# The order of additions and operand sums at the change of passes, and of the left-over rows' weights

## The chip, the cores and the metric

The kernel runs on one core of one Trainium2 chip. A core has five engines, each with its own instruction queue: TensorE (PE, matmuls; PEld is its weight load), VectorE (DVE), ScalarE (ACT), GpSimd (POOL) and SyncE (SP). The last two mostly issue DMAs here; ScalarE issues a few. The metric is the time of one execution on the device in microseconds (us). The profile comes from one such execution.

## The reference

The inputs are x (8 x 5696 x 128), h (5696 x 128) and four weights. First comes a long causal convolution along the sequence, written with FFTs, then a "wave" mixing over tokens and a channel product:

```
y  = irfft(rfft(x, 2S) * rfft(h, 2S))[:, :S]          # S = 5696
th = y @ w_theta
zr, zi = y * cos(th), y * sin(th)
u  = y + w_tok_r @ zr + w_tok_i @ zi                   # token products, S x S weights
out = u + relu(u @ w_ch)
```

Nearly three quarters of the time is the line with the two S x S products.

## The kernel before

**The stages.** The FFT convolution and the phases (theta, sine, cosine, products) take the first part of the span. From about 540 us on, the token mixing runs. The contraction over tokens, together with the real and imaginary part, is cut into two halves p = 0 and p = 1, called *passes* here. Within a pass, the 5696 = 2 x 2816 + 64 rows of the result are visited in 22 *visits* tt = 0 to 21; one visit makes the four 128-row by 512-column tiles of rows tt and 22 + tt, for both halves of the batch. One more visit, written tt = None, makes the last 64 rows: the *left-over* visit. Pass 0 goes 0 to 20, None, 21; pass 1 goes 0, None, 1 to 21 (`pairs`).

**A visit.** The contraction of one pass is 11 operand tiles j = 0 to 10 (`bts`). A visit runs through them in four *parts* (`stretches`) of j = 0 to 2, 3 to 5, 6 to 8 and 9 to 10. Ordinary visits use Strassen's seven products instead of eight: each has its own PSUM bank (tags m0 to m6, constants M2, M6, M7, M5, M1, M3, M4), and the seven are run in the order M3, M4, M5, M2, M1, M7, M6 (`ORDER`, L1290). After the last part, VectorE adds each bank with its sign to the result tiles c11, c12, c21, c22 (L1297), and c goes to a buffer in HBM (pass 0, `cp_hbm`) or to the output stage (pass 1).

**Operand sums.** Strassen's products need sums of the operand blocks b11, b12, b21, b22. For each j there are five, numbered k = 0 to 4 in `sum_ops` (L833 to 838; all show as L835): M3 = b12 - b22, M4 = b21 - b11, M1 = b11 + b22, and then b12 and b21 are overwritten by b11 + b12 and b21 + b22. The first visit of each pass (in pass 0 the second too) is *plain* (`plain`, branch `classic`): eight products with the raw blocks (L1210), so the sums can be made while it runs. The last two of a j must wait until the plain visit has read that j. The left-over visit needs only M3 and M4 of each j (L1178, with the raw b11 and b22); the visits after it need all five. In pass 1 the sums wait in a list `sums_1`, from which `late_sums(n)` issues the first n.

**Weights.** They come as f32 pairs through a ring of six slots, by POOL (L680, `load_w`, called from `pump`, which goes on when `prepare` marks a chunk as read). `prepare(i)` makes the weights of part i: block transposes on VectorE from the ring (`w_t`, L894), then Strassen's sums of weights (`w_sum`, L903). Usually part i + 1 is prepared as part i begins, and at the end of a visit interleaved with the final additions (`woven`), unless the left-over visit comes next. The transposed weights have five slots, the sums four.

**Output stage.** `u_stage` has two halves. `first`: ScalarE casts c to ub (L971), TensorE transposes it into utp (L974), ScalarE copies that to SBUF (L976). `second`: TensorE multiplies by w_ch into v (L981), VectorE makes c + relu(v) (L983), SP stores it. Both PSUM tiles use the bank "misc". The stages of finished tiles wait in `spread`; `aside(first_of, second_of)` issues one half each, once per part.

**Orders.** Tile, the layer below, plans each engine's order from the order of issue and its own cost model. In two stretches of the mixing the order of VectorE is kept as written (`manual_schedule`, `ordered`, L1117 to 1122): at the start of pass 0, and in pass 1 from the first plain part until visit 1 begins. The rest of the text calls these written-out orders. The other engines' orders are always planned.

**At the change of passes before.** In the last plain part of pass 1, six sums are issued ahead of the products (L1241), then the four result additions (L1253), then all sums left (L1269, six), then four more enter the list. In the left-over visit the stage's first half stands ahead of each part's matmuls, its second half behind them, and all remaining sums are issued behind the first part (L1183).

Of the kernel before, what the change touches and what calls it, by code (L numbers as in the profile page):

```python
# [22 lines left out]
def kernel(  # L23
# [624 lines left out]
    first_of = {}  # L648
# [83 lines left out]
    M2, M6, M7, M5, M1, M3, M4 = range(7)  # L732
# [100 lines left out]
    def sum_ops(bt):  # L833
        b11, b12, b21, b22 = (bt[q] for q in (M2, M6, M7, M5))
        return [lambda f=f, x=x: f(*x) for f, x in (  # L835
            (nc.vector.tensor_sub, (bt[M3], b12, b22)), (nc.vector.tensor_sub, (bt[M4], b21, b11)),
            (nc.vector.tensor_add, (bt[M1], b11, b22)), (nc.vector.tensor_add, (b12, b11, b12)),
            (nc.vector.tensor_add, (b21, b21, b22)))]
# [209 lines left out]
    def late_sums(n):  # L1048

        for _ in range(min(n, len(sums_1))):  # L1050
            sums_1.pop(0)()

    stretches = []
    for k, (p, tt, c) in enumerate(chunks):
# [58 lines left out]
            return a  # L1113
        return a, step

    nxt, second, st = None, None, {}
    ordered = ExitStack()  # L1117
    for i, (k, p, tt, j0, s0, nj) in enumerate(stretches):
        if (p, tt, j0 + s0) in ((0, 0, 0), (1, 0, 0)):
# [20 lines left out]
        if p and first_of_pair and tt == 1:  # L1140
            nc.vector.tensor_add(zl[2], zl[0], zl[1])
        if p and tt == 0:
            sums_1 += [op for j in range(nj) for op in sum_ops(bts[j0 + s0 + j])[:3]]
        held = a if i else None
        a, nxt = nxt, None if i == 1 else prepare(i + 1, not woven)
        if woven:
            nxt, step = nxt
        def aside(first_of, second_of):
            nonlocal second
            if first_of and spread and (p == 1 or (tt > 0 and not end_of_pair)):  # L1150
                where_bg["tags"] = ("c2", "c3") if j0 + s0 == TJ else ("red", "mag")
                _, first, second = spread.pop(0)
                with tc.issue_after(sides["late"].ins) if p == 0 and tt == 1 else ExitStack():
                    first()
                    if len(spread) > 1:
                        spread[1][0]()
            if second_of and second is not None:
                second()
                second = None

        if tt is None:
            if p:
                aside(True, False)
            if first_of_pair:
                q = M1 if p else M3
                ps = mps.tile([P, 512], F32, tag=f"m{q}", name=f"m{q}")
                c_last = addend_last(p)
            a1, a2, sa = a
            terms = ((sa, M2, a2, M4), (a1, M3, sa, M5))
            for j in range(nj):  # L1170
                jj = j0 + s0 + j
                for r in range(2):
                    b = [x[:, r, :] for x in bts[jj]]
                    st_ = jj == 0 and r == 0
                    sp_ = jj == NJ - 1 and r == 1 and zl is None
                    for k_ in range(2):
                        for h, t in enumerate(terms):
                            nc.tensor.matmul(ps[64 * h:64 * h + 64], t[2 * k_][:, j, :64, r], b[t[2 * k_ + 1]],  # L1178
                                             start=st_ and k_ == 0, stop=sp_ and k_ == 1)
            if p:  # L1180
                aside(False, True)
            if p == 1:
                late_sums(len(sums_1))  # L1183
            if end_of_pair:
                if zl is not None:
                    wl = wl_room()
                    nc.sync.dma_start(wl[:, :64], wl_hbm[:, NT - 1, :64])
                    for h in range(2):
                        nc.tensor.matmul(ps[64 * h:64 * h + 64], wl[:, :64], zl[h], start=False, stop=True)
                c, c0 = c_last  # L1190
                nc.vector.tensor_add(c, c0, ps)
                finish(p, NT - 1, 0, c)
            continue
# [43 lines left out]
                            sum_some(1)  # L1237
            continue
        if classic:
            if p and end_of_pair:  # L1240
                late_sums(6)  # L1241
            for n in range(4):
                for j in range(nj):
                    product(a, j0 + s0 + j, j, n, range(2))
                    if p == 0 and (n * nj + j) % 4 != 3:
                        sum_some(1)
                if end_of_pair and n % 2:
                    (c12, z12), (c21, z21), (c11, z11), (c22, z22) = cs
                    out_of = (((c11, z11, 0), (c12, z12, 1)), ((c21, z21, 2), (c22, z22, 3)))[n // 2]
                    for h, (c, z, m_) in enumerate(out_of):  # L1250
                        if p:
                            nc.tensor.matmul(ms[m_], wl[n // 2], zl[h], start=False, stop=True)
                            nc.vector.tensor_tensor(c, z, ms[m_], op=add)  # L1253
                            continue
                        if n == 1:
                            nc.tensor.matmul(ms[m_], ident_bf, z, start=False, stop=True)
                        else:
                            for b in range(4):
                                nc.tensor.matmul(ms[m_][:, b * D:(b + 1) * D], z[:, b, :], ident_bf,
                                                 start=False, stop=(b == 3))  # L1260
                        nc.scalar.activation(c, ms[m_], AF.Copy)
                aside(n == 0, n == 2)
            if end_of_pair and woven:
                for n_ in range(7):
                    step(n_)
            if p == 0:
                done["used"] = tt * (j0 + s0 + nj)
            else:
                late_sums(len(sums_1) if end_of_pair else 3)  # L1269
                sums_1 += [op for j in range(nj) for op in sum_ops(bts[j0 + s0 + j])[3:]]  # L1270
        else:
            left = {}
            if zl is not None and end_of_pair:
                left = {M5: (wl[0], zl[1]), M7: (wl[0], zl[2]),
                        M2: (wl[1], zl[0]), M6: (wl[1], zl[2])}
            if end_of_pair:
                (c12, z12), (c21, z21), (c11, z11), (c22, z22) = cs
                sums = {M3: ((c12, z12, add), (c22, z22, add)), M4: ((c11, z11, add), (c21, z21, add)),
                        M5: ((c11, c11, ALU.subtract), (c12, c12, add)),
                        M2: ((c21, c21, add), (c22, c22, ALU.subtract)),  # L1280
                        M1: ((c11, c11, add), (c22, c22, add)),
                        M7: ((c11, c11, add),), M6: ((c22, c22, add),)}
            while owed and owed[0][0] < j0 + s0 + nj:
                sum_some(1)
            for n, q in enumerate(ORDER):
                sum_some(1)
                for j in range(nj):
                    jj = j0 + s0 + j
                    for r in range(2):
                        nc.tensor.matmul(ms[q], a[q][:, j, :, r], bts[jj][q][:, r, :],  # L1290
                                         start=(jj == 0 and r == 0),
                                         stop=(jj == NJ - 1 and r == 1 and q not in left))
                if q in left:
                    nc.tensor.matmul(ms[q], left[q][0], left[q][1], start=False, stop=True)  # L1294
                if end_of_pair:
                    for c, z, op in (sums[q][::-1] if i + 1 == len(stretches) and q == M5 else sums[q]):
                        nc.vector.tensor_tensor(c, z, ms[q], op=op)  # L1297
                    if i + 1 == len(stretches):
                        if n == 4:
                            ends = [u_stage(t, h, c, P) for (t, h), (c, _) in zip(where, cs)]  # L1300
                            ends[0][1]((f"m{M3}", f"m{M5}", "yy0"))
                        elif n == 5:
                            ends[1][1]((f"m{M4}", f"m{M2}", "yy1"))
                        elif n == 6:
                            ends[0][2]()
                            ends[2][1]((f"m{M1}", f"m{M3}", "yy2"))
                            ends[1][2]()
                            ends[3][1]((f"m{M7}", f"m{M5}", "yy3"))
                            ends[2][2]()
                            ends[3][2]()  # L1310
                    if woven:
                        for n_ in {1: (0, 1), 2: (2,), 3: (3,), 4: (4,), 5: (5,), 6: (6,)}.get(n, ()):
                            step(n_)
                aside(n == 1, n == 4)
# [38 lines left out]
```

## Time and profile before

| what | value |
|---|---|
| median of 3 runs | 2037.92 us (2035.97 to 2045.31) |
| profiled execution | 2040.29 us, span 2038.5 us |
| TensorE busy | 1944.0 us, 95% |
| VectorE busy | 1539.8 us, 76% |
| GpSimd busy | 966.7 us, 47% |
| ScalarE busy | 638.9 us, 31% |

In rows of the timeline the first number is the start in us from the span's start, the second the length of the group, then the engine, line and operation, output <- input, the number of instructions and, in brackets, the idle time before the first and what ended it. Rows of waits give the waiting engine and what it waited for, the total in us, the number of times and the longest. The span is from the first to the last instruction; the execution's own time is a little longer.

The change of passes on TensorE lies at 1215 us (visit 21 of pass 0 ends, the plain visit of pass 1 begins), the left-over visits near 1171 and 1260 us.

### The profile page before, as it was taken

How to read it: one execution, taken by the hardware profiler on the slowest of the kernel's cores; microseconds unless marked ns; L12 is line 12 of the kernel's file. 1: busy time of each engine (PE TensorE's matmuls, PEld its weight loads, DVE VectorE, ACT ScalarE, POOL GpSimd, SP SyncE). 2: the span in 40 equal slices, each digit the busy share in tenths (PEclk: the TensorE clock that was granted, in tenths of full speed). 3: DMA queues.
4: the chain of work that ended last, by engine and by line, in shares of the span. 5: the costliest groups of instructions: out<-in, count | busy, mean ns of one | idle time of the engine just before them, and what ended most of it. 6: DMA issues, size and time to landing. Idle time of an engine off the chain costs nothing.

```text
span 2038.5 us, 42418 instructions
## 1 busy us (share of the span) xinstructions
PE 1944.0 (95%) x16121; PEld 1077.9 (53%) x16297; DVE 1539.8 (76%) x2817; ACT 638.9 (31%) x936; POOL 966.7 (47%) x1769
## 2 busy tenths in 40 slices
PE   7789898799999999999999998999999999999998
PEld 5688887654444444444444443444444444444444
DVE  8877877557778787887867668768677786777767
ACT  6788787762233323332300000111111111111111
POOL 8334213284353545454566454553545445354450
PEclk9999999899999999999999999999999999999999
DMA  9999988899798989999999798896978879788793
GB/s 155 163 173 145 161 164 231 244 261 178 157 180 173 174 173 162 181 173 181 165 173 152 122 247 206 137 154 126 153 136 141 151 126 155 130 151 142 134 157 84
DMA packets 510349, 334.77 MB, mean 164 GB/s; under 512 B 186631, under 2 KB 463111, under 8 KB 510055
## 3 DMA queue, kind: packets, MB, share of 16 engines
q0 software_dynamic: 322368, 157.47, 60.6%
q1 hardware_dynamic: 181792, 163.03, 27.3%
q10 hardware_dynamic: 5984, 11.54, 1.6%
q8 instruction: 128, 2.10, 0.4%
q14 instruction: 77, 0.63, 0.1%
HBM read 374.82 MB, written 95.24 MB: 231 GB/s over the span
## 4 chain that ended last, share of the span: by engine, by line
PE 66%; DMA 3%; DVE 3%; issue 1%; POOL 0%; ACT 0%; DVEq 0%
PE m L1290 61%; DMA ring<-in_moe_w_tok_i_dram 3%; DVE c L1297 1%; PE utp L974 1%; PE v L981 1%; PE m L1294 1%; DVE wt L894 1%; DMA ring<-in_moe_w_tok_r_dram 1%; PE theta_ps L564 0%; DVE b L835 0%; PE tpz L922 0%; PE m L1178 0%; POOL ring L680 0%; ACT ub L971 0%; DVE c L983 0%
## 5 line engine op out<-in xcount | busy, mean ns | idle before, releaser
L680 POOL DMA_DIRECT2D ring<-in_moe_w_tok_i_dram x720 | 388.6, 545 | 663.0 <-DVE wt L894 583.8
L680 POOL DMA_DIRECT2D ring<-in_moe_w_tok_r_dram x720 | 387.2, 546 | 130.2 <-DVE wt L894 70.9
L894 DVE STREAM_TRANSPOSE wt<-ring 128x384 f32<-128x384 f32 (+2 forms) x720 | 359.9, 525 | 115.6 <-PE m L1290 81.3
L1290 PE MATMUL m<-b,wt 128*128 128x512 bf16 x1604 | 384.8, 379 | 3.8 <-DVE wt L894 1.7
L1290 PEld LDWEIGHTS <-wt 128*128 128x128 bf16 x1804 | 176.0, 98 | 215.4 <-DVE wt L894 3.9
L1297 DVE TENSOR_TENSOR c<-c,m 128x512 f32<-128x512 f32 x412 | 265.9, 671 | 0.4 <-PE m L1290 0.4
L976 ACT ACTIVATE ring<-utp 128x512 bf16<-128x512 bf16 x85 | 50.7, 597 | 577.5 <-PE utp L974 577.5
L453 PE MATMUL ps<-r_u,uv_t 128*128 128x128 f16 x1024 | 117.3, 220 | 5.4 <-DVE g__1416 L460 2.0
L1210 PE MATMUL m<-b,wt 128*128 128x512 bf16 x471 | 113.0, 387 | 8.8 <-DMA b<-z_hbm 4.8
L971 ACT ACTIVATE ub<-c 128x512 bf16<-128x512 f32 x88 | 55.1, 628 | 201.0 <-DVE c L1253 118.6
L454 PE MATMUL ps<-r_v,uv_t 128*128 128x100 f16 x1024 | 115.3, 209 | 0.1
L153 POOL DMA_DIRECT2D x<-in_x_dram x128 | 99.5, 783 | 20.4 <-POOL x L151 14.9
L454 PEld LDWEIGHTS <-uv_t 128*128 128x128 f16 x1024 | 100.8, 99 | 5.9 <-issue 4.9
L433 DVE TENSOR_TENSOR uv_t<-xs,hs 128x2048 f16<-128x2048 f16 x77 | 91.5, 1223 | 16.3 <-DMA hs<-hf_hbm 9.2
L453 PEld LDWEIGHTS <-uv_t 128*128 128x128 f16 x1024 | 100.9, 98 | 2.3 <-DVE uv_t L438 2.1
L431 ACT ACTIVATE xs<-ps 128x1024 f16<-128x1024 f32 x96 | 90.8, 972 | 30.1 <-PE ps L270 14.3
L1210 PEld LDWEIGHTS <-wt 128*128 128x128 bf16 x528 | 51.5, 100 | 71.0 <-issue 12.6
L566 ACT ACTIVATE red<-theta_ps,magic 128x512 f32<-128x512 f32 (+1 forms) x46 | 31.6, 687 | 155.6 <-PE theta_ps L564 86.2
L270 PEld LDWEIGHTS <-w_t 64*128 64x128 f16 x3240 | 56.3, 98 | 31.0 <-issue 22.7
L924 ACT ACTIVATE ring<-tpz 128x512 bf16<-128x512 bf16 (+1 forms) x46 | 27.5, 597 | 134.0 <-PE tpz L922 120.2
L250 PE MATMUL ps<-f_t,x 89*128 89x180 f16 x512 | 62.0, 250 | 2.2 <-DVE a L257 1.8
L983 DVE SCALAR_TENSOR_TENSOR c<-v,c 128x512 f32<-128x512 f32 x88 | 60.1, 684 | 4.8 <-PE v L981 4.5
(2925 smaller groups left out, 3733.9 us busy)
## 6 DMA issues: line engine op xcount, KB each, us to landing
ring<-in_moe_w_tok_r_dram POOLq DMA_DIRECT2D x352, 96.0 KB, 4.4
ring<-in_moe_w_tok_i_dram POOLq DMA_DIRECT2D x352, 96.0 KB, 5.0
ring<-in_moe_w_tok_r_dram POOLq DMA_DIRECT2D x352, 80.0 KB, 4.6
ring<-in_moe_w_tok_i_dram POOLq DMA_DIRECT2D x352, 80.0 KB, 3.9
cp_hbm<-c SPq DMA_DIRECT2D x88, 256.0 KB, 2.5
c<-cp_hbm SPq DMA_DIRECT2D x88, 256.0 KB, 4.5
out_dram<-c SPq DMA_DIRECT2D x88, 256.0 KB, 4.7
hs<-hf_hbm SPq DMA_DIRECT2D x77, 256.0 KB, 3.5
```

The source lines that it names most:

```text
L153: nc.gpsimd.dma_start(x16[p0:p1, e, n0:n0 + 16, :HD], bass.AP(tensor=src.tensor, offset=src.offset + (p0 * N2 + n0) * D + dh * HD, ap=[[N2 ...
L250: nc.tensor.matmul(ps[:, i // 2, (i % 2) * 2 * K1:(i % 2 + 1) * 2 * K1], lhs(q + i), f1_t[:NB], start=True, stop=True)
L431: nc.scalar.activation(xs[:, :, :, :ck], ps, AF.Copy)
L433: nc.vector.tensor_tensor(uv[:, :, :, c0:c0 + ck], xs.rearrange("p e d k -> p e (d k)").unsqueeze(1).to_broadcast([P, 2, 2, HD * CK]), hv. ...
L453: nc.tensor.matmul(o, u_t[:, at:at + P], r_u, start=True, stop=False)
L454: nc.tensor.matmul(o[:, 2 * NP:], v_t[:, at:at + P], r_v, start=False, stop=True)
L680: nc.gpsimd.dma_start(wb[32 * i:32 * i + 32, :ng, :nj * 64], bass.AP(tensor=a.tensor, offset=a.offset + row0 * S + p * H + i * QR + j0 * 6 ...
L894: nc.vector.transpose(wt.rearrange("p j t r -> p (j t r)").bitcast(F32).rearrange("p (j g t) -> p g j t", j=TJ, g=4)[:, :ng, :nj], wb[:, : ...
L983: nc.vector.scalar_tensor_tensor(c[:m], v[:m], 0.0, c[:m], op0=ALU.max, op1=ALU.add)
L1210: nc.tensor.matmul(ms[n // 2 * 2 + h], a[n][:, j, :, r], bts_of[p][jj][n % 2 * 2 + h][:, r, :], start=(n % 2 == 0 and jj == 0 and r == 0), ...
L1290: nc.tensor.matmul(ms[q], a[q][:, j, :, r], bts[jj][q][:, r, :], start=(jj == 0 and r == 0), stop=(jj == NJ - 1 and r == 1 and q not in left))
L1297: nc.vector.tensor_tensor(c, z, ms[q], op=op)
```

## The change

It has three parts.

1. In the last plain part of pass 1 the six sums ahead of the products and the flush behind them are gone. Two sums are issued between the two pairs of result additions. In the left-over visit two are issued behind each part; ahead of a part, `needed` issues what that part must have (k < 2 there). Visit 1 issues two ahead of each part while any are left, and `needed` sees that all five are made up to that part's last j. With the sums as listed, that gives: two between the additions, two behind each of the left-over parts, three more ahead of the fourth, two ahead of visit 1's first part and the last ahead of its second.
2. In the left-over visit of pass 1 the output stage's first half moves behind the matmuls of the part's first j, and its v gets the bank of M7 instead of "misc".
3. In pass 0, in the last part of visit 20, part two of the left-over visit is prepared after the product M1 and its additions, ahead of M7 and M6, and kept in `ahead`; before, it was prepared when the left-over visit's first part began. Its ring loads are issued with it.

```
 def late_sums(n):
     for _ in range(min(n, len(sums_1))):
-        sums_1.pop(0)()
+        sums_1.pop(0)[2]()
+def needed(hi, k):
+    while any(o[0] < hi and o[1] < k for o in sums_1):
+        late_sums(1)
+def sums_of(j, lo, hi):
+    return [(j, k, f) for k, f in enumerate(sum_ops(bts_of[1][j]))][lo:hi]
...
     if p and tt == 0:
-        sums_1 += [op for j in range(nj) for op in sum_ops(bts[j0 + s0 + j])[:3]]
+        sums_1 += [op for j in range(nj) for op in sums_of(j0 + s0 + j, 0, 3)]
+    if p and tt is None:
+        needed(j0 + s0 + nj, 2)
+    elif p and tt:
+        late_sums(2)
+        needed(j0 + s0 + nj, 5)
-    a, nxt = nxt, None if i == 1 else prepare(i + 1, not woven)
+    a, nxt = nxt, None if i == 1 else ahead.pop(i + 1) if i + 1 in ahead else prepare(i + 1, not woven)
-    def aside(first_of, second_of):
+    def aside(first_of, second_of, *banks):
...
-                first()
+                first(*banks)
...
     if tt is None:
-        if p:
-            aside(True, False)
...
+            if p and j == 0:
+                aside(True, False, ("misc", f"m{M7}", None))
         if p:
             aside(False, True)
-        if p == 1:
-            late_sums(len(sums_1))
+            late_sums(2)
...
     if classic:
-        if p and end_of_pair:
-            late_sums(6)
...
                         nc.vector.tensor_tensor(c, z, ms[m_], op=add)
+                        late_sums(2 if n == 1 and h else 0)
...
-            late_sums(len(sums_1) if end_of_pair else 3)
-            sums_1 += [op for j in range(nj) for op in sum_ops(bts[j0 + s0 + j])[3:]]
+            late_sums(0 if end_of_pair else 3)
+            sums_1 += [op for j in range(nj) for op in sums_of(j0 + s0 + j, 3, 5)]
...
             if end_of_pair:
+                if n == 4 and p == 0 and not woven and i + 2 < len(stretches):
+                    ahead[i + 2] = prepare(i + 2)
```

More of the change, by code (lines that the diff above doesn't have):

```diff
@@ L1114, in prepare @@
         return a, step
-    nxt, second, st = None, None, {}
+    nxt, second, st, ahead = None, None, {}, {}
     ordered = ExitStack()
```

## The prediction

> **What bounds the kernel now.** I began with the page: span, busy shares and the chain that ended last.
>
> ```profile
> span 2038.5 us, 42418 instructions
> PE 1944.0 (95%) x16121; PEld 1077.9 (53%) x16297; DVE 1539.8 (76%) x2817; ACT 638.9 (31%) x936; POOL 966.7 (47%) x1769
> PE 66%; DMA 3%; DVE 3%; issue 1%; POOL 0%; ACT 0%; DVEq 0%
> ```
>
> TensorE is busy 95% of the span and carries 66% of the chain. So a microsecond is won only where TensorE itself stands still or runs slowly, and the next view is what TensorE waits for, once from 1160 to 1300 us (both edited places) and once from 1300 us to the end.
>
> ```profile
> PE utp L974 <- ACT ub L971: 3.4, 1, 3.4
> PE m L1210 <- DMA b<-z_hbm: 1.8, 2, 1.1
> PE m L1178 <- DVE out__18210 L903: 1.1, 1, 1.1
> ...
> PE utp L974 <- ACT ub L971: 0.9, 2, 0.7
> PE v L981 <- ACT uts L976: 0.2, 1, 0.2
> ```
>
> The first three rows are the early window, the last two all that it waits for after 1300 us: 1.1 us in 738. What is won at the change of passes is therefore kept to the end, as long as that order holds. The busy times by stretch (length; then PE, PEld, DVE, ACT, POOL; then the granted clock) show the place:
>
> ```profile
> 1247.00:1253.00 6.00, 4.20 (x20) 1.85 (x20) 6.00 (x12) 0.00 (x0) 3.71 (x8) 1.00 0.86 142
> 1253.00:1256.40 3.40, 3.37 (x16) 1.34 (x14) 3.40 (x9) 0.00 (x0) 1.30 (x3) 1.00 1.14 152
> 1256.40:1259.70 3.30, 0.00 (x0) 0.00 (x0) 3.30 (x7) 0.61 (x1) 0.00 (x0) 0.88 0.21 35
> 1259.70:1265.50 5.80, 5.73 (x28) 2.31 (x28) 5.07 (x10) 2.17 (x5) 1.06 (x2) 0.50 0.01 3
> ```
>
> VectorE is full while TensorE has nothing to do for 3.3 us, and then TensorE works 5.8 us at a granted clock of 0.50. The instructions of VectorE there, in order of time:
>
> ```profile
> 1253.90 0.34 DVE L903 TENSOR_TENSOR out__18917<-wt 128x384 bf16<-128x384 bf16 x1
> 1254.16 3.69 DVE L835 TENSOR_TENSOR b<-b 128x1024 bf16<-128x1024 bf16 x6
> 1257.78 2.47 DVE L1253 TENSOR_TENSOR c<-c,m 128x512 f32<-128x512 f32 x4
> 1260.17 3.69 DVE L835 TENSOR_TENSOR b<-b 128x1024 bf16<-128x1024 bf16 x6
> 1263.78 0.63 DVE L894 STREAM_TRANSPOSE wt<-ring 128x192 f32<-128x192 f32 x2
> 1264.44 0.36 DVE L903 TENSOR_TENSOR out__18991<-wt 128x384 bf16<-128x384 bf16 x1
> 1266.13 0.69 DVE L983 SCALAR_TENSOR_TENSOR c<-v,c 128x512 f32<-128x512 f32 x1 [1.33 <-PE v L981]
> ...
> 1274.10 0.69 DVE L983 SCALAR_TENSOR_TENSOR c<-v,c 128x512 f32<-128x512 f32 x1 [2.59 <-PE v L981]
> 1274.71 1.49 DVE L894 STREAM_TRANSPOSE wt<-ring 128x384 f32<-128x384 f32 x3
> ```
>
> and of TensorE, with two rows of ScalarE:
>
> ```profile
> 1255.77 0.59 PE L1252 MATMUL m<-zl,wl 128*128 128x512 bf16 x2
> 1259.77 0.61 PE L974 MATMUL utp<-ident_bf,ub 128*128 128x128 bf16 x4 [3.41 <-ACT ub L971]
> 1270.22 0.41 PE L1178 MATMUL m<-b,out__19043 128*64 128x512 bf16 x1 [0.35 <-DVE out__19043 L903]
> ...
> 1271.56 0.38 PE L1178 MATMUL m<-b,out__19043 128*64 128x512 bf16 x2
> 1271.78 0.38 PE L1178 MATMUL m<-b,wt 128*64 128x512 bf16 x2
> ...
> 1273.60 0.40 PE L981 MATMUL v<-w_ch_sb,ring 128*128 128x128 bf16 x4
> 1273.93 0.41 PE L1178 MATMUL m<-b,out__19096 128*64 128x512 bf16 x1
> ...
> 1277.34 0.38 PE L1290 MATMUL m<-ring,wt 128*128 128x512 bf16 x1 [0.16 <-DVE wt L894]
> ```
>
> ```profile
> 1259.09 0.63 ACT L971 ACTIVATE ub<-c 128x512 bf16<-128x512 f32 x1 [118.61 <-DVE c L1253]
> 1260.48 0.60 ACT L976 ACTIVATE ring<-utp 128x512 bf16<-128x512 bf16 x1 [0.76 <-PE utp L974]
> ```
>
> TensorE ends the plain visit at 1255.77 + 0.59 = 1256.36. Six operand sums (1254.16, 3.69 us) hold VectorE until the four additions start at 1257.78; the first output tile needs one, ScalarE's copy needs that, and the transposes on TensorE need the copy. The first part's matmuls, whose operand was ready at 1254.24, stand behind those transposes. The left-over rows end, and visit 1 begins, at 1277.34: **20.98 us** after the plain visit.
>
> **The change, part by part.**
>
> *Additions ahead of sums.* VectorE free at 1254.24 (1253.90 + 0.34) adds two results at 2.47/4 = 0.62 us each, to 1255.5, makes two sums at 3.69/6 = 0.615 each, to 1256.7, and adds the other two, whose matmuls end at 1256.36, to 1258.0. ScalarE's copy (0.63) then ends near 1256.2, before TensorE is free.
>
> *The output stage moves behind the first j of each part.* The matmuls on two column halves start at once at 1256.36, and the 4 transposes, ScalarE's 0.60 copy, the 4 matmuls into v, the 0.69 update of c and its output DMA on SP follow. The j after the first take two times four pairs at 1271.78 - 1271.56 = 0.22, 1.7 us, which covers the 0.60 copy. So no idle 3.41 us, and with it no 5.8 us at half clock. A part runs in 1273.93 - 1270.22 = 3.71 us at full clock (stage included), and the last, shorter one with the zl rows in 1277.34 - 1273.93 = 3.41. Three times 3.71 plus 3.41 is 14.5 against 20.98: **6.4 us** if nothing else waits. v has its own bank, m2 by tag, which visit 1 needs only as its sixth or fifth product; nothing waits for it there.
>
> *Preparing parts two to four.* Two transposes and a sum, 0.63 + 0.36 = 1.0 us each, end near 1259.0, 1263.0 and 1266.5 (after the update of c and two sums of the part before), against TensorE's needs at 1260.1, 1263.8 and 1267.5: covered by 0.8 us or more. The ring loads on POOL that follow these transposes go out some 5 us earlier, into a stretch that now shows a DMA share of 0.01 to 0.21: costs nothing.
>
> *The new wait.* The sums spread two to a part, each pair behind that part's update of c, which waits for v at the part's end. So the first two sums that the last part needs ((9,0), (9,1)) start only when TensorE has finished part three, and three more ((9,2), (10,0), (10,1)) stand ahead of j = 10. From TensorE's end of part three: update 0.65, sums to 1.4 and 2.0, j = 9 (its three later pairs) to 2.65, transposes to 3.05, (10,1) at 3.85, j = 10 to 4.5. Unhindered, j = 10 would end at 0.86 + 0.40 + 0.86 = 2.1. **Cost 2.4 us**; the ends are 0 (the matmuls of M2 and the transposes fill it) and 3.7 (all five sums plus the update, nothing beside them). I take the worked-out 2.4.
>
> *Visit 1.* Its weights' transposes start at +3.85 and M3 is ready 0.5 later, before TensorE is through (+5.8): hidden. Behind them, though, two late sums now stand ahead of the addition of the left-over rows, whose bank M1 is wanted again:
>
> ```profile
> 1281.20 0.56 DVE L903 TENSOR_TENSOR out__19153<-wt 128x768 bf16<-128x768 bf16 x1 [0.26 <-PE m L1290]
> 1281.68 0.68 DVE L983 SCALAR_TENSOR_TENSOR c<-v,c 128x512 f32<-128x512 f32 x1
> 1282.28 0.68 DVE L1191 TENSOR_TENSOR c_last<-c_last,m 128x512 f32<-128x512 f32 x1
> ...
> 1283.02 0.61 PE L1290 MATMUL m<-ring,out__19149 128*128 128x512 bf16 x2
> ```
>
> The M6 operand waits for a slot that the M5 product frees, so this chain keeps its distance to the visit's start: M1 could begin 1283.02 - 1277.34 = 5.7 us in, and now 1.23 later, at 6.9. The fifth product is due at 5 and M7 (1.3) can go ahead of it as far as the planner sees it. **Cost 0.6** (6.9 less 5 + 1.3), ends 0 and 1.9. The last three sums go beside visit 1; VectorE's 1.9 us lie under its idle time (page: 76% busy).
>
> *Left-over rows of pass 0.*
>
> ```profile
> 1169.20 4.87 DVE L1297 TENSOR_TENSOR c<-c,m 128x512 f32<-128x512 f32 x8
> 1173.98 0.89 DVE L894 STREAM_TRANSPOSE wt<-ring 128x192 f32<-128x192 f32 x3
> 1174.80 0.32 DVE L903 TENSOR_TENSOR out__18210<-wt 128x384 bf16<-128x384 bf16 x1
> ```
>
> Part two's preparation stands behind eight additions, two of which (M7, M6: 2 x 0.61 = 1.2 us) it now passes; the 1.1 us wait of the third row of waits goes. Its eight ring loads on POOL go out 1.2 us earlier too; the two passed additions and their stores to cp on SP come 0.9 later, with their banks wanted no sooner than visit 21's sixth product. But ahead lies the wait of 1.8 us for b from z_hbm at the start of pass 1, and a TensorE that comes earlier may only wait longer there. Ends 0 and 1.1; both are the same distance off, and I take the middle, **0.5**.
>
> Sum: 6.4 - 2.4 - 0.6 + 0.5 = **3.9 us gained**. The profiled execution took 2040.29 us with a span of 2038.5; its own would be 2036.4. It stood 2.4 above the median shown, 2037.92, from which the forecast follows: **2034.0 us**.
>
> [...] The row shows 5.8 us at 0.50 after 3.41 idle, and 1.00 through two waits of 1.1 and 0.7 (1247 to 1253). [...]
>
> **The rivals.**
>
> *The clock falls anyway.* The last part's waits of 2.4 us lie close together; if they drop the clock as 3.41 did, 5.8 us of it give half, 2.9 us, away: 1.0 gained, 2036.9. For: the same kind of wait. Against: the clock stayed at 1.00 over 1.8 us of waits within 4. Chance 0.08. [...]
>
> *The wait only moves.* The planner keeps M1 in place (1.9 in place of 0.6), the last part takes its upper end (3.7), pass 0's gain is lost to b: 6.4 - 3.7 - 1.9 = 0.8 gained, 2037.1. For: VectorE is full through the whole change. Against: its list as worked out has idle time while it waits for v. Chance 0.14.
>
> *The waits vanish.* Only VectorE's order is written out here, so TensorE's may put other matmuls ahead of those that wait: 6.4 + 1.1 = 7.5 gained, 2030.4. Against: part four has no other matmuls than those named. Chance 0.11.
>
> *Slower: the planner's order in pass 1 shifts.* From visit 1 on the order is the planner's, and it starts from another state. Its place is each following visit, where an operand's sum could come late as at 1270.22 (wait 0.35): 21 such visits cost 7.4 us, less 3.9, so 3.5 slower, 2041.4. It decides from 0.19 us a visit on, and to be over 0.5% slower it takes 0.67. For: nothing fixes that order. Against: TensorE waits 1.1 us in all those visits together, and VectorE has a quarter of its time free. Chance 0.13.
>
> **How the numbers follow.** Forecast (2 to 6 gained) 0.54, waits vanish 0.11, wait moves 0.14, clock 0.08, slower 0.13. The predicted 2034.0 is the first case's, whose own range is 2032 to 2036. The range of all runs from 2029 (every wait gone, 6.4 + 1.1 + the 1.1 of later waits = 8.6) to 2040 (about half of the slower case), some 0.9 of the chance with a share for how runs scatter (2035.97 to 2045.31). A measurement of this kernel tells about 0.5%, 10 us, from no change, and no case but a large planner shift reaches that: faster 0.03, same 0.92, slower 0.05.
>
> **What would show it.** In the profile after: no wait of utp for ub near the plain visit's end; the clock at 1.00 in the left-over rows; a wait of the L1178 line's matmuls for the operand sums in the last part, about 2 us in total; visit 1 starting near 17 us after the plain visit instead of 20.98; a small wait of an M1 matmul for c_last; no wait for the second part's sum in pass 0, and a wait for b at least as long as 1.8. Wrong would be: a clock below 1.00 after the plain visit, or waits after 1300 us well above 1.1.

## The result and the profile after

Over 22 runs of each kernel the changed one takes 2033.66 us in the median (2027.65 to 2042.13) and the kernel before 2039.43 (2030.5 to 2046.05). The ratio is 0.9974 with a 95% interval of 0.9961 to 0.9986: 0.0026 x 2039.43 = 5.3 us gained, 2.9 to 8.0. The forecast was 2034.0, from 3.9 gained.

The profiled execution shows almost none of that: 2039.61 us with a span of 2037.8, against 2040.29 and 2038.5. Within these 22 runs single executions of one kernel lie up to 16 us apart, so the place of the change has to be read by itself. What TensorE waits for between 1160 and 1300 us, in the kernel after (total us, times, longest):

```profile
PE m L1222 <- DMA b<-z_hbm: 2.4, 1, 2.4
PE m L1301 <- DVE c_last L1203: 2.0, 1, 2.0
PE v L981 <- DVE b L835: 0.7, 1, 0.7
PE m L1189 <- DVE b L835: 0.4, 2, 0.2
...
PE m L1189 <- DVE out__18196 L903: 0.3, 1, 0.3
```

The 3.4 us for `ub` are gone. In their place stand two longer waits at other places (L1222 are the plain products of pass 1, L1301 the products of visit 21 in pass 0, L1203 the addition of the left-over rows), 0.3 us for the weights `out__18196` at the left-over visit of pass 0, and 1.16 us for operand sums in the last left-over part, where 2.4 were forecast. The same place by stretches (length; PE, PEld, DVE, ACT, POOL; granted clock, DMA share, GB/s):

```profile
1249.90:1252.20 2.30, 0.00 (x0) 0.00 (x0) 2.30 (x6) 0.00 (x0) 1.10 (x3) 1.00 0.90 171
1252.20:1256.60 4.40, 4.32 (x13) 1.69 (x13) 1.72 (x5) 0.00 (x0) 3.04 (x6) 0.62 1.00 131
...
1261.00:1271.40 10.40, 10.40 (x97) 4.85 (x96) 7.44 (x17) 3.35 (x6) 5.15 (x10) 1.00 0.70 106
```

The third row is the gain: TensorE is busy for all of the first three left-over parts, at a clock of 1.00. The first two rows are a loss: in this execution b came late from HBM within the plain visit, and behind 2.39 us of idle the clock fell (0.62 is the mean of the second row). VectorE and TensorE after, in order of time:

```profile
1256.97 1.28 DVE L1263 TENSOR_TENSOR c<-c,m 128x512 f32<-128x512 f32 x2 [3.04 <-PE m L1262]
1258.17 1.29 DVE L835 TENSOR_TENSOR b<-b 128x1024 bf16<-128x1024 bf16 x2
1260.85 1.29 DVE L1263 TENSOR_TENSOR c<-c,m 128x512 f32<-128x512 f32 x2 [1.40 <-PE m L1262]
...
1271.61 0.69 DVE L983 SCALAR_TENSOR_TENSOR c<-v,c 128x512 f32<-128x512 f32 x1 [0.86 <-PE v L981]
1272.22 3.09 DVE L835 TENSOR_TENSOR b<-b 128x1024 bf16<-128x1024 bf16 x5
...
1282.88 0.68 DVE L1203 TENSOR_TENSOR c_last<-c_last,m 128x512 f32<-128x512 f32 x1
```

```profile
1260.43 0.59 PE L1262 MATMUL m<-zl,wl 128*128 128x512 bf16 x2
1260.96 0.41 PE L1189 MATMUL m<-ring,out__18917 128*64 128x512 bf16 x1
...
1264.45 0.40 PE L1189 MATMUL m<-b,out__18981 128*64 128x512 bf16 x1
...
1271.44 0.40 PE L1189 MATMUL m<-b,out__19086 128*64 128x512 bf16 x1
...
1272.92 0.40 PE L981 MATMUL v<-w_ch_sb,ring 128*128 128x128 bf16 x4 [0.75 <-DVE b L835]
...
1274.76 0.38 PE L1189 MATMUL m<-b,wt 128*64 128x512 bf16 x1 [0.18 <-DVE b L835]
1275.37 0.38 PE L1189 MATMUL m<-b,wt 128*64 128x512 bf16 x1 [0.23 <-DVE b L835]
...
1276.58 0.38 PE L1301 MATMUL m<-ring,wt 128*128 128x512 bf16 x1 [0.16 <-issue]
...
1283.12 0.38 PE L1301 MATMUL m<-ring,out__19148 128*128 128x512 bf16 x1
...
1283.62 0.60 PE L1301 MATMUL m<-ring,out__19144 128*128 128x512 bf16 x2
```

VectorE now waits for TensorE (3.04, 1.40 us) and no longer the other way round. The plain visit ends at 1260.43 + 0.59 = 1261.02, and visit 1 begins at 1276.58, **15.56 us** later, where it was 20.98. The rest of the difference between the two profiled executions can be laid out by stretches of TensorE:

| stretch | before | after | difference |
|---|---|---|---|
| start of pass 0's left-over visit | 1171.27 | 1172.52 | +1.25 |
| left-over visit and visit 21 of pass 0 | 44.18 | 45.47 | +1.29 |
| plain visit of pass 1 | 40.91 | 43.03 | +2.12 |
| left-over visit of pass 1 | 20.98 | 15.56 | -5.42 |
| start of visit 1 | 1277.34 | 1276.58 | -0.76 |

The first row lies ahead of nearly every edit, and executions of one kernel differ there by more (1171.27 and, in before_again below, 1161.91). The third is the late b, 2.39 - 1.80 = 0.59, and the slow clock behind it. From 1300 us on TensorE still waits 0.9 + 0.2 = 1.1 us, as before, and its busy time from 1300 to 1900 us is 596.68 us in both: what the change of passes wins is kept to the end.

### The profile page after: what moved, and what is told of

It reads as the page before. It is cut to its first block, busy times and chain, and to the rows that moved or that the text cites. A ratio compares the mean times of both kernels' runs of the same rounds, so it can differ in the third digit from the quotient of the medians.

```text
span 2037.8 us, 42414 instructions
## 1 busy us (share of the span) xinstructions
PE 1945.8 (95%) x16121; PEld 1079.8 (53%) x16297; DVE 1537.4 (75%) x2817; ACT 639.2 (31%) x936; POOL 964.6 (47%) x1769
## 4 chain that ended last, share of the span: by engine, by line
PE 64%; DMA 3%; DVE 2%; POOL 2%; issue 2%; ACT 0%; DVEq 0%; ACTq 0%; POOLq 0%
PE m L1301 60%; DMA b<-z_hbm 2%; POOL ring L680 1%; DVE c L1308 1%; DMA ring<-in_moe_w_tok_r_dram 1%; PE v L981 1%; PE utp L974 1%; PE m L1305 1%; PE m L1189 1%; DVE wt L894 1%; PE theta_ps L564 0%; PE tpz L922 0%; PE m L1222 0%; POOL wl L941 0%; DMA ring<-in_moe_w_tok_i_dram 0%
## 5 line engine op out<-in xcount | busy, mean ns | idle before, releaser
L1301 PE MATMUL m<-b,wt 128*128 128x512 bf16 x1604 | 384.6, 379 | 3.8 <-DVE wt L894 1.7
L1301 PEld LDWEIGHTS <-wt 128*128 128x128 bf16 x1804 | 176.0, 98 | 217.7 <-DVE wt L894 4.3
L1222 PE MATMUL m<-b,wt 128*128 128x512 bf16 x471 | 114.6, 391 | 12.4 <-DMA b<-z_hbm 7.0
L1222 PEld LDWEIGHTS <-wt 128*128 128x128 bf16 x528 | 51.7, 100 | 74.1 <-issue 14.0
```

What stands on the lines that cost most here:

```text
L1222: nc.tensor.matmul(ms[n // 2 * 2 + h], a[n][:, j, :, r], bts_of[p][jj][n % 2 * 2 + h][:, r, :], start=(n % 2 == 0 and jj == 0 and r == 0), ...
```

## The experiments

The times of a few us are near what runs can resolve. So the kernels are judged first by the lengths of the same four stretches, in one profiled execution each. The first of them repeats to 0.01 us where the kernels agree in what leads up to it.

| kernel | left-over and visit 21, pass 0 | plain visit | of it waiting for b | plain visit's end to visit 1 |
|---|---|---|---|---|
| before | 44.18 | 40.91 | 1.80 | 20.98 |
| before_again | 44.18 | 40.09 | 0.76 | 19.34 |
| before_warm | 44.18 | 40.05 | 0.88 | 20.22 |
| stage_only | 44.17 | 41.24 | 2.13 | 21.29 |
| only_ahead | 45.20 | 39.70 | 0.54 | 17.93 |
| sums_only | 44.18 | 41.80 | 2.73 | 15.74 |
| no_ahead | 44.18 | 40.47 | 1.30 | 15.33 |
| after | 45.47 | 43.03 | 2.39 | 15.56 |
| after_again | 43.91 | 41.08 | 1.91 | 15.91 |
| by_need | 45.23 | 39.57 | 0.41 | 17.75 |
| by_need2 | 43.78 | 42.88 | 2.02 | 13.75 |
| by_need3 | 44.18 | 39.86 | 0.46 | 13.75 |

(In before_warm the filler's 3.45 us are counted in the last column and not in the plain visit.) Less its wait for b, the plain visit is 39.1 to 39.4 us in all rows but after and by_need2, where the clock fell within it.

**One part alone.** sums_only has the first part of the change, with the output stage left at the head of each part and no early preparation; stage_only and only_ahead are the kernel before with the second and the third part. Their edits are those parts of the diff above, unaltered; the one that takes the stage back is

```
     if tt is None:
+        if p:
+            aside(True, False)
...
-            if p and j == 0:
-                aside(True, False, ("misc", f"m{M7}", None))
```

> The spread of the sums and the additions ahead of them, with the output stage left at the head of each left-over part and without the early preparation in pass 0. My theory: the additions' place does nearly all of it, since the transposes at the head find their copy ready when TensorE ends the plain visit; from the plain visit's end to visit 1's start 15.6 to 16.5 us (20.98 before, 15.62 with the whole change), the clock at 1.00 in the left-over rows. Rival: the stage's move is needed as well, because the transposes still stand ahead of the first part's matmuls; then 18 us or more and a slow clock. Time: 3 to 6 us under the kernel before.

> Only the output stage moves behind the first j of each left-over part, with its own bank for v; the sums stand as before. My theory: 0.9 us of matmuls fill the wait of 3.4, which leaves 2.5 of idle time. If 2.5 us are enough to drop the clock (a wait of 2.39 did so in the changed kernel's plain visit), the distance from the plain visit's end to visit 1 is about 20.1 us; if the clock holds, about 17.4. Rival: the stage's move alone does the work: 16.5 or less. Time: 1 to 3.5 us under the kernel before.

> Only the early preparation of part two of the left-over visit in pass 0. Both theories: the left-over visit of pass 0 takes 10.3 us in place of 11.16, and the change of passes stays at 21.0 with the slow clock. First theory: the 2.0 us that visit 21 then waited for the left-over rows' addition (behind weights still under way) come from the earlier preparation, and return here: no gain, or a loss of 1. Rival: that wait is the DMAs' scatter from execution to execution; here it may be 0 to 2, and the time is 0 to 1 us under the kernel before.

Against 2037.65 us of the kernel before (28 runs), sums_only took 2033.17 (10 runs; ratio 0.9983, 0.9971 to 0.9995), stage_only 2037.46 (0.9999, 0.9982 to 1.0016) and only_ahead 2037.01 (0.9999, 0.9981 to 1.0016). The first part alone brings 20.98 down to 15.74, within 0.2 us of the whole change. The second alone gains nothing: 21.29, longer than either length that was expected. The third alone shows 17.93, with a clock that did not fall, where 21.0 and a slow clock were expected; the reasons follow below. Here is VectorE and then TensorE in stage_only:

```profile
1256.68 3.69 DVE L835 TENSOR_TENSOR b<-b 128x1024 bf16<-128x1024 bf16 x6
1260.29 2.47 DVE L1253 TENSOR_TENSOR c<-c,m 128x512 f32<-128x512 f32 x4
1262.68 3.69 DVE L835 TENSOR_TENSOR b<-b 128x1024 bf16<-128x1024 bf16 x6
1266.30 0.62 DVE L894 STREAM_TRANSPOSE wt<-ring 128x192 f32<-128x192 f32 x2
1266.95 0.36 DVE L903 TENSOR_TENSOR out__18991<-wt 128x384 bf16<-128x384 bf16 x1
```

```profile
1262.28 0.61 PE L974 MATMUL utp<-ident_bf,ub 128*128 128x128 bf16 x4 [3.92 <-ACT ub L971]
...
1268.16 0.38 PE L974 MATMUL utp<-ident_bf,ub 128*128 128x128 bf16 x4 [0.75 <-ACT ring L976]
1268.47 0.40 PE L1176 MATMUL m<-b,out__18991 128*64 128x512 bf16 x1
```

With the six sums still ahead of the additions, the transposes come as late as before. TensorE has the first j's matmuls to do, about 1 us of work, then waits 3.92. `out__18991`, behind the second six, is ready at 1266.95 + 0.36 = 1267.31, but the second part begins only at 1268.47: TensorE's planner put the transposes of two more tiles ahead of it, and the later ones wait 0.75 us for ScalarE's copy out of their bank (and 0.74 once more ahead of the third part). What the stage's move would give without these 1.5 us of waits, no run shows.

**Does the slow clock cost what the forecast gave it?** The forecast put 6.4 us down to 3.4 of idle and 2.9 for the half-rate stretch behind it. before_warm gives TensorE unread matmuls to do in that idle time of the kernel before, to measure the distance without the slow clock; it adds work that nothing reads. If the slow clock cost 2.9 us, the distance from the plain visit's end to visit 1 comes down to 20.98 - 2.9 = 18.1 us.

```
     if tt is None:
+        if p and first_of_pair:
+            fill = mps.tile([P, 512], F32, tag=f"m{M7}", name="fill")
+            for n in range(16):
+                nc.tensor.matmul(fill, ident_bf, zl[0], start=True, stop=True)
```

> The kernel before with 16 matmuls of 512 columns at the left-over visit's head in pass 1, into the bank of M7, which nothing reads: 3.5 us of TensorE's work in the place of its wait, so that the clock has no reason to fall. [...] Rival: the distance is VectorE's, and the clock cost nothing on the path: it stays at 20 to 21.

> The kernel before once more. The wait of the transposes for the copy should be 1.5 to 4 us, with 21 us from the plain visit's end to visit 1 where the clock falls and about 18 where it holds; no wait for the left-over rows' addition in visit 21 of pass 0.

before_warm took 2043.5 us in its single execution, before_again 2028.73, beside 2035.1 of the kernel before (13 runs), so their times decide nothing. The traces do. The 20.22 us of before_warm in the table's last column are what the rival said; but that length also depends on when the plain visit ends, so VectorE's own work is the better measure. First VectorE in before_warm, then TensorE:

```profile
1258.84 3.69 DVE L835 TENSOR_TENSOR b<-b 128x1024 bf16<-128x1024 bf16 x6
...
1269.11 0.36 DVE L903 TENSOR_TENSOR out__18991<-wt 128x384 bf16<-128x384 bf16 x1
```

```profile
1264.44 0.40 PE L974 MATMUL utp<-ident_bf,ub 128*128 128x128 bf16 x4 [0.86 <-ACT ub L971]
...
1269.53 0.41 PE L1182 MATMUL m<-b,out__18991 128*64 128x512 bf16 x1 [1.65 <-DVE out__18991 L903]
...
1280.35 0.61 PE L1294 MATMUL m<-ring,wt 128*128 128x512 bf16 x2
```

With the clock at 1.00 (all of 1255 to 1272 us) TensorE is sooner through the first part, and then waits 1.65 us for the second part's weights. In only_ahead the clock held without a filler (1.00 from 1251.97 to 1262 us; its wait for `ub` was 1.79 us), and the same 1.65 us appear (TensorE, then VectorE's first set of six sums):

```profile
1253.76 0.40 PE L974 MATMUL utp<-ident_bf,ub 128*128 128x128 bf16 x4 [1.79 <-ACT ub L971]
1258.85 0.40 PE L1178 MATMUL m<-b,out__18991 128*64 128x512 bf16 x1 [1.65 <-DVE out__18991 L903]
...
1269.90 0.38 PE L1290 MATMUL m<-ring,wt 128*128 128x512 bf16 x1 [0.16 <-DVE wt L894]
```

```profile
1248.15 3.69 DVE L835 TENSOR_TENSOR b<-b 128x1024 bf16<-128x1024 bf16 x6
```

In before_again the clock did fall, but for a shorter time (the last section has the lengths). VectorE's first set and TensorE's first product of visit 1 there:

```profile
1243.78 3.69 DVE L835 TENSOR_TENSOR b<-b 128x1024 bf16<-128x1024 bf16 x6
```

```profile
1265.52 0.61 PE L1290 MATMUL m<-ring,wt 128*128 128x512 bf16 x2
```

So VectorE paced this place. From the start of the first six sums to the end of `out__18991` it takes 1269.11 + 0.36 - 1258.84 = 10.63 us in before_warm, 1266.95 + 0.36 - 1256.68 = 10.63 in stage_only, and 1264.44 + 0.36 - 1254.16 = 10.64 in the kernel before, whatever the clock. From the same start to visit 1 it is 21.5 us in before_warm (1280.35 - 1258.84), 21.75 in only_ahead (1269.90 - 1248.15), 21.74 in before_again (1265.52 - 1243.78) and 23.2 in the profiled execution of before (1277.34 - 1254.16). In that execution the slow clock was worth the difference, 1.4 to 1.7 us; in before_again, where it was half as long (3.41 us against 6.83), it was worth nothing. What TensorE would gain beyond that it would lose to the wait for VectorE. It also shows why the last column of the table scatters for the kernels with the old order (17.93 to 21.29): TensorE's end of the plain visit moves with b, VectorE's chain does not follow it.

**Sums by need.** In the list of sums the three of one j stand together, though the left-over visit wants only two. by_need sorts the list so that those two come first for every j.

```
     if classic:
+        if p and end_of_pair:
+            sums_1.sort(key=lambda o: o[1] >= 2)
```

> The whole change, with the waiting sums of the plain visit's last part put in the order of need (the two of j = 9 and 10 that the left-over visit uses come first). My theory: the 1.1 us that the fourth left-over part waited for sums go, and nothing else moves: 14.5 us from the plain visit's end to visit 1 in place of 15.6. Rival: the part waits for the stage's chain (cast, transposes, copy, product) anyway, and stays at 15.3 or more. Time: about 1 us under the changed kernel, which the rounds can't tell.

> The changed kernel once more, for the scatter of its trace. If the wait for the left-over rows' addition in visit 21 belongs to the early preparation, it is 1.7 to 2.0 us here too (1.99 in the first trace, 1.71 and 1.75 in the two other kernels with that preparation, none in the three without). If it is scatter, it may be absent. The wait for b from z_hbm should fall anywhere from 0.4 to 2.7 us, and the distance from the plain visit's end to visit 1 should be near 15.6 us where TensorE comes late, longer where that wait is short, since VectorE's additions then come late for it.

by_need took 2030.7 us (7 runs; against 2037.65: 0.9976, 0.9956 to 0.9996), after_again 2034.57 in its single execution. In by_need no wait for sums is left in the last part, as meant, but, against what was expected, the old wait is back: 2.01 us for `ub`, 1.76 for the copy behind it, 17.75 from the plain visit's end to visit 1. VectorE shows why:

```profile
1249.48 1.28 DVE L835 TENSOR_TENSOR b<-b 128x1024 bf16<-128x1024 bf16 x2
1250.69 1.28 DVE L1265 TENSOR_TENSOR c<-c,m 128x512 f32<-128x512 f32 x2
1251.88 2.49 DVE L835 TENSOR_TENSOR b<-b 128x1024 bf16<-128x1024 bf16 x4
1254.29 1.27 DVE L1265 TENSOR_TENSOR c<-c,m 128x512 f32<-128x512 f32 x2
```

The sums that nobody needs before visit 1 were now issued in visit 1, behind the end of the written-out order. There they are the planner's, and it put two of them ahead of the first additions and two more between the pairs, which is the arrangement the change does away with. by_need2 keeps the sorted list and issues them within the written-out order: three behind each of the first three left-over parts, and the rest behind the addition of the left-over rows.

```
-                late_sums(2)
+                late_sums(0 if end_of_pair else 3)
             if end_of_pair:
...
                 nc.vector.tensor_add(c, c0, ps)
+                if p:
+                    late_sums(len(sums_1))
```

> The whole change with the sums in the order of need, three behind each of the first three left-over parts, and the rest in the written-out order behind the addition of the left-over rows, so that none is left for the planner to pull ahead of the result additions (in the run by need it put two more ahead of them and two more between them). My theory: the transposes at the plain visit's end wait as in the changed kernel (not at all where TensorE comes late, under 1 us where it comes early), the fourth part waits for nothing, and visit 1 begins 14.5 to 15.5 us after the plain visit. Rival: VectorE's three sums a part make the weights of the next part late, and the gain goes there. Time: 1 to 2 us under the changed kernel.

It took 2032.1 us (10 runs) against 2035.1: 0.998, 0.9962 to 0.9998. The last column falls to 13.75 with a single wait of 0.18 us left, 0.75 less than the 14.5 that the forecast had for no wait at all.

**Without the early preparation.** The table's first column is 44.17 or 44.18 in all seven executions without the third part. With it, it is 45.20, 45.47 and 45.23 in three and 43.91 and 43.78 in two. no_ahead is the changed kernel without it, by_need3 is by_need2 without it.

```
-                    if n == 4 and p == 0 and not woven and i + 2 < len(stretches):
-                        ahead[i + 2] = prepare(i + 2)
```

> The whole change without the early preparation in pass 0. My theory by now: that part gives nothing, since what the left-over visit of pass 0 gains (0.9 us) comes back as visit 21's wait for the left-over rows' addition (0.3 to 2.0 us in the five traces with it) and as the plain visit's wait for b from z_hbm. So visit 21 shows no such wait, the left-over visit of pass 0 takes 11.16 us, and the time is that of the changed kernel or up to 1 us less: a ratio of 0.996 to 0.999. Rival: the early preparation carries part of the gain; the ratio is above that, 0.999 or more.

> The sums in the order of need, three to a part, as in by_need2, and without the early preparation in pass 0. My theory: both gains stand side by side: 13.8 to 15 us from the plain visit to visit 1, no wait for the left-over rows' addition in visit 21; 1 to 2 us under the whole change, ratio 0.995 to 0.998. Rival: the end of the plain visit is set by b's arrival, and VectorE's sums by TensorE, so that the two don't add: ratio 0.998 or more.

Against 2035.91 us (22 runs), no_ahead took 2031.35 (12 runs; 0.9979, 0.996 to 0.9998) and by_need3 2031.07 (12 runs; 0.9973, 0.9953 to 0.9992). The waits of TensorE in no_ahead from 1160 to 1300 us:

```profile
PE m L1222 <- DMA b<-z_hbm: 1.3, 1, 1.3
PE m L1189 <- DVE out__18210 L903: 1.1, 1, 1.1
...
```

and in by_need3:

```profile
PE m L1189 <- DVE out__18210 L903: 1.1, 1, 1.1
PE m L1224 <- DMA b<-z_hbm: 0.5, 1, 0.5
PE m L1305 <- DVE wt L894: 0.2, 1, 0.2
```

The 1.1 us for `out__18210` are back, and the wait of visit 21 for `c_last` is gone. Its chain in the kernel after, first VectorE and then TensorE:

```profile
1183.80 0.58 DVE L894 STREAM_TRANSPOSE wt<-ring 128x384 f32<-128x384 f32 x1 [2.46 <-DMA ring<-in_moe_w_tok_i_dram]
...
1184.89 0.68 DVE L1203 TENSOR_TENSOR c_last<-yy_last,m 128x512 f32<-128x512 bf16 x1
```

```profile
1185.62 0.59 PE L1301 MATMUL m<-ring,wt 128*128 128x512 bf16 x2 [1.99 <-DVE c_last L1203]
```

VectorE waits 2.46 us for a ring load of visit 21's weights, the addition of the left-over rows is queued behind that transpose, and visit 21 wants that addition's bank. The same chain stands in all five executions with early preparation, with 1.99, 1.71, 1.75, 0.43 and 0.30 us of TensorE's wait (after, only_ahead, by_need, after_again, by_need2). So the third part wins 0.9 us in the left-over visit of pass 0 (the 1.1 us for `out__18210` less the 0.3 for `out__18196`, which the kernel before doesn't have) and gives 0.3 to 2.0 back one visit later. That transpose runs without a wait and ahead of visit 21 in the kernel before. Why the load lands later in these five is open: on POOL it is issued about 1.2 us earlier, counted from the left-over visit's start (2.18 against 3.38). SP's stores of c are in flight beside it, but no run separated the two.

by_need2 and by_need3 have the shortest left-over visit in pass 1, and no_ahead lacks the third part, but their times can't be told from that of the changed kernel: all intervals overlap. So whether the third part gives or takes is left open by the times.

## Why the prediction was right

The forecast time was 2034.0 us and the median 2033.66; the interval of the gain, 2.9 to 8.0 us, holds the forecast 3.9. That the two times are so close is luck: over 22 runs the kernel before has a median 1.5 us above the 2037.92 that the forecast started from, and the gain is 1.4 us larger than forecast. Step by step:

- *Additions ahead of sums: 20.98 to 14.5, if nothing else waits.* Right in size: 20.98 to 15.56 with 1.16 us of waits, and 13.75 once the sums come by need. Each left-over part runs in 3.5 us (1264.45 - 1260.96 = 3.49) and not in 3.71: the row used for that length has the transposes behind five matmuls, where they now stand behind eight, and takes 0.22 us more, the time of one pair of matmuls; no run tests whether that is the reason. Wrong in its account: of the 6.4 us, 2.9 were put down to the slow clock. That was worth 1.4 to 1.7 in the profiled execution and nothing in before_again. The rest, which the forecast didn't name, was that VectorE's second six sums would have held the second part anyway. The sum came out because the change moves both sets of six sums, those ahead of the additions and those behind them; a change that had only kept TensorE's clock up would have been forecast 1.2 us or more too well.
- *The stage behind the first j.* It was counted in with the first step. Alone it gives nothing, and on top of the first part it takes 15.74 to 15.33 (no_ahead), in one execution each.
- *Preparing parts two to four: covered.* Right: no wait for these weights is left.
- *The new wait for sums, 2.4.* Right in place and kind, 1.16 in size (0.75 + 0.18 + 0.23). The last part took 1276.58 - 1271.44 = 5.14 us where 3.41 + 2.4 = 5.81 were worked out. The forecast had v's transposes and products at their places in the list; TensorE's planner let them run into the wait.
- *M1's bank, 0.6.* M1 began 1283.62 - 1276.58 = 7.04 us into visit 1, where 6.9 was forecast, but TensorE waited for nothing: the planner put not only M7 but three of M6's matmuls too ahead of it. The first part of visit 1 took 9.72 us, before 9.66. Cost 0.06.
- *Pass 0's early preparation, +0.5.* Wrong in mechanism. The wait for `out__18210` went, as said. What followed was not only a longer wait for b but, at once, visit 21's wait for `c_last`: -1.29 in the profiled execution, +0.27 in after_again. The step looked at the ring loads as "1.2 us earlier" and took that to be harmless.
- *The rivals.* The clock did not fall in the last left-over part (1.00 from 1261.00 to 1276.50 us); it fell in the plain visit behind a wait of 2.39 us for b, which neither the forecast nor a rival had. The row of the slow clock "after 3.41 idle" was itself read too simply: in the kernel before the fall came 2.55 us into the wait of 3.41 (last section). "The waits vanish" was half true of the last part. No sign of a planner that drifts: 1.1 us of waits after 1300 us, as forecast.

So two costs were sized too high (by 1.2 and 0.5 us) and the early preparation's gain of 0.5 was not there, which would make 3.9 + 1.2 + 0.5 - 0.5 = 5.1. A finer account isn't to be had: the left-over visit alone gained 20.98 - 15.56 = 5.4 us in one pair of executions and 19.34 - 15.91 = 3.4 in the other, by how late b came and how long the slow clock lasted.

## What to carry to other kernels

Put what another engine waits for ahead of sums that no one needs yet, and look at which engine paces the place: filling TensorE's idle time to keep its clock up was worth 1.7 us at most while VectorE's own chain of 10.6 us set the next part. Where an order is written out only for a stretch, work that is moved out of the stretch can be planned back into it; issue it inside, at its end. An operation won on one visit has to be followed until the next place where the same queue is waited for.

## What had not been expected of the hardware

In these traces the clock's fall does not follow the length of the idle time alone. It fell to 0.50 behind 3.41 us (before), 3.92 (stage_only) and 3.21 (before_again), but also behind 2.39 (after) and 2.02 (by_need2), and it held at 1.00 through 2.73 us in sums_only. All changes of the granted clock in the traces of before (25) and after (23) lie on a grid of steps of 3.413 us (to within 0.003 us), which starts at another point in each of the two; here an execution's grid is continued through the stretches without a change. What tells the cases apart is the idle time within one such step. Here are two steps of by_need2 and three of sums_only (columns as above):

```profile
1247.46:1250.87 3.41, 1.39 (x7) 0.57 (x6) 3.41 (x7) 0.00 (x0) 2.10 (x4) 1.00 0.92 195
1250.87:1254.28 3.41, 3.41 (x9) 1.22 (x8) 3.41 (x7) 0.00 (x0) 2.68 (x5) 0.50 0.69 83
```

```profile
1239.71:1243.12 3.41, 2.26 (x11) 1.02 (x11) 3.41 (x7) 0.00 (x0) 1.73 (x4) 1.00 1.15 295
1243.12:1246.53 3.41, 1.83 (x8) 0.78 (x8) 3.41 (x7) 0.00 (x0) 2.10 (x4) 1.00 0.47 74
1246.53:1249.94 3.41, 3.41 (x17) 1.56 (x16) 3.41 (x9) 0.63 (x1) 2.21 (x5) 1.00 1.08 147
```

The 2.02 us of by_need2 lie in one step (3.41 - 1.39), in which 1.39 us of work did not hold the clock: the next one runs at 0.50. The 2.73 us of sums_only are cut by the grid into 1.15 and 1.58, and the clock stays at 1.00. Five steps behind 545 us have 2.02 us of idle or more: by_need2 (2.02), stage_only (2.27), after (2.39), before (2.55) and before_again (3.21). Each was followed by a fall. The wait of 1.91 us in after_again was not (1.00 from 1246.5 to 1252 us), and in before and after no other step from 545 to 2010 us has over 1.49 us of idle or a fall behind it. Earlier in the span, with other work, falls follow steps with as little as 1.06 us (after, 102.94 to 106.35 us), so these numbers hold for this stretch only. The slow time lasts one step (3.41 us) in after, by_need2 and before_again, where TensorE is busy all through it, and two steps (6.83 us) in before and stage_only, where the first of them still has 0.9 and 1.7 us of idle in it.

With the clock down, the twelve matmuls behind the wait for b took 4.38 us in the kernel after; in sums_only, at 1.00, they took 2.87. So the wait of 2.39 us in the kernel after cost 1.5 us more.
